# Two decode attentions on one core: the last sum in four strips with two stores, and the last rows of wo in three transfers

## The chip, the cores and the metric

The kernel runs on one core of a Trainium2 chip. Its time is the device time in microseconds of one launch. A run is also profiled; all durations below are of that one profiled execution, and they are compared with its own time.

## The reference

Two independent problems A and B of the same shape are computed and their results set side by side. Each is a decode step of attention with one query per batch entry: B = 2, D = 576, 32 query heads, 16 key/value heads of 128, a cache of 16384 positions of which the last W = 4096 are used.

```python
q = (x @ wq).reshape(B, 1, 32, 128).transpose(0, 2, 1, 3)
k = repeat(k_cache[:, :, Sk - W:, :], 2, axis=1)
v = repeat(v_cache[:, :, Sk - W:, :], 2, axis=1)
p = softmax(einsum("bhqd,bhkd->bhqk", q, k) * 128 ** -0.5)
o = einsum("bhqk,bhkd->bhqd", p, v)
return o.transpose(0, 2, 1, 3).reshape(B, 1, 4096) @ wo      # (2, 1, 576)
```

The output is `concatenate([a, b], axis=-1)`, bf16 of shape (2, 1, 1152). All inputs are bf16. The caches that are read, 4 times 33.5 MB, are nearly all of the 153 MB that the kernel moves.

## The kernel before

The kernel writes each engine's instruction order out by hand: `S.add(engine, fn, deps)` appends to that engine's list, and the dependencies become semaphore waits. All big transfers are issued by SyncE in one list, `stream`: wq of both problems, then per step one slab of K and one of V (4 MB each, for one group of heads of both batch entries), with the parts of wo set between them by `issue_wo`. A ring of four slabs, `ring`, takes them; a slab is issued when the slab four places earlier has been read.

A step `D_` (16 of them, `ND`, eight per problem) handles two key/value heads, one per batch entry: VectorE transposes the K slab into `xt` (L515), TensorE multiplies it with the masked queries `zq` into a score buffer `ST` (L540 and L188, which is the second matmul on weights that are already loaded), ScalarE takes the exponential (L585), VectorE transposes that into `pC` (L593), and TensorE multiplies `pC` with the V slab into `ACC` (L631, in four column strips of 32). Two steps make a group `G` (8 of them, `NG`), and a group's normalised output is multiplied with its rows of wo in `do_proj`. For all groups but the last (`by_group`), 512 of the 576 output columns are summed in PSUM tile `OT`, the other 64 in VectorE's `o_rest`.

The end of the kernel is the last group (`G` = 7, steps 14 and 15). `issue_slab` sends the last V slab in two pieces (L252), then `issue_wo(3)` the four head slices of step 14 (L291, 576 KB), and `issue_last` the rows of wo for the four heads of step 15: `HEADS = [(0, 1), (2,), (3,)]`, one transfer each of 288, 144 and 144 KB (L277), all into `wob`, each with its own semaphore `wl_sem`. All of these were issued by 332.3 us and wait in the transfer queues behind the slabs. Then SyncE issues the store of A's result `out_A` (L831), and last that of B's.

Before the last group, the sum so far is copied out of `OT` and `o_rest` into a part of a free score buffer, `fin(0)` (partitions 0 and 1, columns 0 to 287) and `fin(1)` (partitions 32 and 33, columns 512 to 799): `fin0` by ScalarE (L810), `fin1` and `fin2` by VectorE (L811, L813). The last group's matmuls add to it:

```python
for half in range(2):
    last = e.matmul(fin(half), l_, wob[:, w0 + s_, half * NH:(half + 1) * NH],
                    start=False, stop=end, skip_group_check=True)
```

Those of step 14 wait for `fin_ops`; those of step 15 are three parts (L778), each waiting for its own transfer of wo. In between stand three idle matmuls (`do_redist(3, 3)`), which compute nothing that is used. `do_E` then copies one half to bf16 by ScalarE (L822) and the other by VectorE (L823), both into `pR`, and `do_out` (L831) stores the two rows of 576 columns when both copies are done. SyncE waits for the stores (L985).

Of the kernel before, what the change touches and what calls it, by code (L numbers as in the profile page):

```python
# [7 lines left out]
ACTF = mybir.ActivationFunctionType  # L8
ALU = mybir.AluOpType
# [50 lines left out]
def build_kernel(nc, probs, out, cfg=None):  # L60
# [8 lines left out]
    NPROB = len(probs)  # L69
    Bb, _one, D = x0.shape  # L70
# [12 lines left out]
    ND = SPP * NPROB  # L83
# [5 lines left out]
    HH = HD // 2  # L89
    NXC = NFC + 2  # L90
    NOUT = wo0.shape[1]
    NH = NOUT // 2
    NB0 = 512
    NB1 = NOUT - NB0
    assert NOUT % 2 == 0 and 0 < NB1 <= NB0
    SCALE = float(Dh) ** -0.5
    ZW = 152
    BIG = -1.0e30
# [3 lines left out]
    NSW = 32  # L102
    unit_of = {G: u for u, (g0, n) in enumerate(UNITS) for G in range(g0, g0 + n)}
    HEADS = [(0, 1), (2,), (3,)]
    NPC = len(PIECES)

    def by_group(G):
        return G < NG - 1

    def wo_slot(G):  # L110
        return {0: 0, 1: 8, 2: 16, 3: 24, 4: 0, 5: 8, 6: 16, 7: 24}[G]

    es = ExitStack()
    with es:
# [3 lines left out]
        wob = sb("wob", [128, NSW, NOUT], BF16)  # L118
# [21 lines left out]
        pR = sb("pR", [128, 1024], BF16)  # L140
# [24 lines left out]
        o_rest = sb("o_rest", [Bb, NB1], FP32)  # L165
        ident_r = sb("ident_r", [128, 32], BF16)
        out_A = sb("out_A", [Bb, NOUT], BF16)
        out_sb = [out_A[:, :], pR[0:Bb, 0:NOUT]]
        ps = lambda name, shape: es.enter_context(nc.psum_tensor(name, shape, FP32))
        NTB = 2  # L170
        TB = [ps("tb%d" % i, [128, 512]) for i in range(NTB)]
        ST = [ps("st%d" % i, [128, 1024]) for i in range(2)]
        OT = ps("ot", [128, 512])
# [7 lines left out]
        x_sem = sem("xload")  # L181
        wl_sem = [sem("wl%d" % n_) for n_ in range(len(HEADS))]
        out_sem = sem("outdone")
        piece_sem = [sem("piece%d" % n_) for n_ in range(NPC)]

# [7 lines left out]
        S = _Sched()  # L193
        dma_count = {}

        def dma_op(eng, sem_h, n_dmas, fn, deps, tag):
            op = S.add(eng, fn, deps, tag)
            dma_count[sem_h] = dma_count.get(sem_h, 0) + 16 * n_dmas
            op.dma = (sem_h, dma_count[sem_h])
            return op  # L200
# [33 lines left out]
        wo_last = []  # L234
        qproj = {}
        proj = {}
# [34 lines left out]

        def issue_last(woP, lo, r0, deps):
            for n_, hs in enumerate(HEADS):
                def f(e, n_=n_, hs=hs):
                    t, r = divmod(hs[0], 2)
                    row = t * HH + r0 + 256 + 128 * r
                    return e.dma_start(wob[:, lo + 4 + hs[0]:lo + 4 + hs[0] + len(hs), :],  # L277
                                       woP[row:row + 128 * len(hs), :].rearrange("(h d) n -> d h n", d=128)).then_inc(wl_sem[n_], 16)
                wo_last.append(dma_op("sp", wl_sem[n_], 1, f, deps, "wl%d" % n_))

        def issue_wo(part):
            lo, n, r0, P, deps, Gs = (
# [42 lines left out]
        rest_add = {}  # L325
# [4 lines left out]
        e_ops = {}  # L330
# [429 lines left out]

        fin_ops = []

        def fin(half):
            return ST[(ND - 2) % 2][32 * half:32 * half + Bb, 512 * half:512 * half + NH]

        def do_proj(D_):
            G = D_ // 2
            P = G // GPP
            u = unit_of[G]
            s0 = 8 * (G - UNITS[u][0])  # L770
            w0 = wo_slot(G)
            new = G % GPP == 0
            if by_group(G):
                parts = [([(Rsb[u % 2][:, :, s0 + s_], s_) for s_ in range(8)], [r_ev[u], wo_dma[G]], new, True, True)]
            elif D_ < ND - 1:
                parts = [([(Rsb[u % 2][:, :, s_], s_) for s_ in range(4)], [r_ev[u], wo_dma[G]] + fin_ops, False, False, False)]
            else:
                parts = [([(oTn[:, h, :], 4 + h) for h in hs], [norm[D_], wo_last[n_]], False, False, n_ == len(HEADS) - 1)  # L778
                         for n_, hs in enumerate(HEADS)]
            for lhs, deps, start, rstart, rstop in parts:  # L780
                def f(e, rest, lhs=lhs, start=start, rstart=rstart, rstop=rstop):
                    last = None
                    for n_, (l_, s_) in enumerate(lhs):
                        begin, end = n_ == 0, n_ == len(lhs) - 1
                        if by_group(G):
                            first = e.matmul(OT[0:Bb, 0:NB0], l_, wob[:, w0 + s_, 0:NB0], start=start and begin, stop=end, skip_group_check=True)  # L786
                            last = matmul_again(e, first, rest[0:Bb, 0:NB1], wob[:, w0 + s_, NB0:NOUT], rstart and begin, rstop and end)
                        else:
                            for half in range(2):
                                last = e.matmul(fin(half), l_, wob[:, w0 + s_, half * NH:(half + 1) * NH],  # L790
                                                start=False, stop=end, skip_group_check=True)
                    return last
                deps = deps + [e_ops[(P - 1, 0)]]
                if by_group(G):
                    n, bank, proj[D_] = tb_job(f, "proj%d" % D_, deps)
                    rest_at[G] = bank
                    if G % GPP < GPP - 1 and G < NG - 2:
                        d = [proj[D_]]
                        if new:
                            if P:  # L800
                                d.append(e_ops[(P - 1, 1)])
                            rest_add[G] = S.add("dve", lambda e: e.tensor_copy(o_rest[:, :], bank[0:Bb, 0:NB1]), d, "rest%d" % G)
                        else:
                            d.append(rest_add[G - 1])
                            rest_add[G] = S.add("dve", lambda e: e.tensor_tensor(o_rest[:, :], o_rest[:, :], bank[0:Bb, 0:NB1], ALU.add),
                                                d, "rest%d" % G)
                        tb_consumer[n] = rest_add[G]
                    elif G == NG - 2:
                        d = [proj[D_], chain[(ND - 2, "exp")], chain[(ND - 2, "max")]]
                        a_ = S.add("act", lambda e: e.activation(fin(0), OT[0:Bb, 0:NH], ACTF.Copy), d, "fin0")  # L810
                        tb_consumer[n] = S.add("dve", lambda e: e.tensor_tensor(  # L811
                            fin(1)[:, NB0 - NH:NH], o_rest[:, :], bank[0:Bb, 0:NB1], ALU.add), d + [rest_add[G - 1]], "fin1")
                        fin_ops.append(S.add("dve", lambda e: e.tensor_copy(fin(1)[:, 0:NB0 - NH], OT[0:Bb, NH:NB0]), [a_], "fin2"))  # L813
                    else:
                        rest_at[G] = (n, bank)
                else:
                    proj[D_] = S.add("pe", lambda e, f=f: f(e, None), deps, "proj%d" % D_)

        def do_E(P):
            G = (P + 1) * GPP - 1  # L820
            if G == NG - 1:
                e_ops[(P, 0)] = S.add("act", lambda e: e.activation(out_sb[P][:, 0:NH], fin(0), ACTF.Copy), [proj[2 * G + 1]], "Elo%d" % P)  # L822
                e_ops[(P, 1)] = S.add("dve", lambda e: e.tensor_copy(out_sb[P][:, NH:NOUT], fin(1)), [proj[2 * G + 1]], "Ehi%d" % P)  # L823
                return
            n, bank = rest_at[G]
            e_ops[(P, 1)] = tb_consumer[n] = S.add("dve", lambda e: e.tensor_tensor(
                out_sb[P][:, NB0:NOUT], o_rest[:, :], bank[0:Bb, 0:NB1], ALU.add), [proj[2 * G + 1], rest_add[G - 1]], "Ehi%d" % P)
            e_ops[(P, 0)] = S.add("act", lambda e: e.activation(out_sb[P][:, 0:NB0], OT[0:Bb, 0:NB0], ACTF.Copy), [proj[2 * G + 1]], "Elo%d" % P)

        def do_out(P, c0, c1, eng, deps):  # L830
            dma_op(eng, out_sem, 1, lambda e: e.dma_start(  # L831
                out[:, 0, P * NOUT + c0:P * NOUT + c1], out_sb[P][:, c0:c1]).then_inc(out_sem, 16), deps, "out%d_%d" % (P, c0))

        init_mask()
        for i in range(NG // 2):
# [13 lines left out]
        for s in range(ND):  # L849
            D2 = s - 2  # L850
            c = s - 1
# [29 lines left out]
            if s in proj_at:  # L881
                do_proj(2 * proj_at[s] + 1)
                if proj_at[s] == GPP - 1:
                    do_E(0)
# [20 lines left out]
        do_comb(D_)  # L905
        do_norm(D_)
        do_proj(2 * 5 + 1)
        do_redist(2)
        do_comb(ND - 2)
# [9 lines left out]
        do_proj(ND - 2)  # L919
        do_proj(D_)  # L920
        do_E(NPROB - 1)
        for P in range(NPROB):
            do_out(P, 0, NOUT, "sp", [e_ops[(P, 1)], e_ops[(P, 0)]])

        S.check()

        for e in ENGS:
            n = 0
# [15 lines left out]
        while left:  # L944
            for e in ENGS:
                while idx[e] < len(S.ops[e]):
                    op = S.ops[e][idx[e]]
# [76 lines left out]
```

## Time and profile before

| | us |
|---|---|
| three runs | 362.78, 362.88, 363.33 (median 362.88) |
| the profiled execution | 363.02 |
| its span, first to last instruction | 361.8 |
| TensorE, VectorE, ScalarE, GpSimd busy | 218.6, 200.9, 68.2, 35.3 |
| transfers: 153.27 MB | 424 GB/s over the span |

How to read the views: in the slices of the page each digit is a share in tenths of one of 40 equal stretches of the span. In the chain of waits each line is a start, a duration, and the work (or the transfer) that the end of the kernel was waiting for at that time. In the timeline a line is start, duration, engine, source line, operation, destination and source with shape, number of instructions, and in brackets the idle time before and what ended it; `SPq` and `ACTq` are SyncE's and ScalarE's queues issuing transfers, `PEld` the weight loads of TensorE.

### The profile page before, as it was taken

To read this page: it belongs to the slowest core of one execution; us is meant where nothing else is said; L and a number is where in the kernel's file an instruction comes from. 1 tells how busy PE (TensorE), PEld (TensorE's weight loads), DVE (VectorE), ACT (ScalarE), POOL (GpSimd) and SP (SyncE) were. 2 spreads that over 40 slices of the span, in tenths; PEclk is the share of its full clock that TensorE was granted. 3 is DMA by queue.
4 is the path that set the end of the run, shared out by engine and by line. 5 is a ranking of instruction groups with operands and counts; after the bars stand their busy time and mean duration, and the time that the engine had idled before them with its cause. 6 is when DMAs were issued, how large, how long until landed. Compare 5 with 4: busy or idle time off the path is not lost.

```text
span 361.8 us, 2730 instructions
## 1 busy us (share of the span) xinstructions
PE 218.6 (60%) x1318; PEld 55.8 (15%) x945; DVE 200.9 (56%) x175; ACT 68.2 (19%) x149; POOL 35.3 (10%) x55
## 2 busy tenths in 40 slices
PE   0399195763747207466574737766867707657786
PEld 0010021120111101112120201212121201211132
DVE  4112599846647019283756658392919239079931
ACT  1036502130203002103020203020201203002131
POOL 1000000004000400001300040002100040200020
PEclk9999689997889857969698978899898978969999
DMA  8999999999999999999999999999999999999996
GB/s 348 421 449 406 464 406 437 431 408 453 415 442 438 428 424 438 429 428 438 417 446 422 435 428 442 426 435 428 424 424 440 431 424 433 431 438 428 438 409 248
DMA packets 6491, 153.27 MB, mean 424 GB/s; under 512 B 712, under 2 KB 1232, under 8 KB 1616
## 3 DMA queue, kind: packets, MB, share of 16 engines
q1 hardware_dynamic: 6476, 153.10, 98.8%
q8 instruction: 9, 0.15, 0.2%
q14 instruction: 2, 0.02, 0.0%
q10 hardware_dynamic: 4, 0.00, 0.0%
HBM read 153.10 MB, written 0.00 MB: 423 GB/s over the span
## 4 chain that ended last, share of the span: by engine, by line
DMA 72%; DVE 17%; PE 7%; ACT 3%; SPq 1%; issue 0%
DMA ring<-in_B_k_cache_dram 34%; DMA ring<-in_A_k_cache_dram 27%; DVE xt L515 14%; DMA wob<-in_B_wo_dram 8%; DMA wob<-in_B_x_dram 3%; PE st L188 3%; PE st L540 3%; ACT wob L465 1%; DVE wob L475 1%; ACT qk L483 1%; PE st L450 1%; DVE m L550 1%; ACT wob L470 1%; DVE nM L563 0%; SPq L252 0%
## 5 line engine op out<-in xcount | busy, mean ns | idle before, releaser
L515 DVE STREAM_TRANSPOSE xt<-ring 128x2048 f32<-128x2048 f32 x64 | 145.3, 2284 | 86.6 <-DMA ring<-in_A_k_cache_dram 49.8
L540 PE MATMUL st<-xt,zq 128*128 128x512 bf16 x256 | 111.6, 436 | 122.6 <-DVE xt L515 98.1
L188 PE MATMUL st<-xt,zq 128*128 128x512 bf16 x256 | 110.1, 430 | 0.0
L540 PEld LDWEIGHTS st<-xt,zq 128*128 128x128 bf16 x256 | 27.1, 106 | 216.3 <-DVE xt L515 113.5
L631 PE MATMUL acc<-ring,pC 128*32 128x512 bf16 x512 | 32.5, 381 | 1.2 <-DMA ring<-in_B_v_cache_dram 1.2
L568 ACT ACTIVATE nMrep<-nM 1x128 f32<-1x128 f32 x16 | 4.9, 308 | 146.9 <-DVE nM L563 146.9
L643 ACT ACTIVATE acc_sb<-acc 128x512 bf16<-128x512 f32 x16 | 9.5, 596 | 79.9 <-PE acc L631 79.9
L593 DVE STREAM_TRANSPOSE pC<-pR 128x1024 bf16<-128x1024 bf16 x16 | 19.6, 1223 | 3.7 <-ACT pR L585 2.1
L650 POOL TENSOR_TENSOR acc_sb<-acc_sb,masks 128x1024 bf16<-128x1024 bf16 (+1 forms) x8 | 13.4, 1679 | 66.6 <-ACT acc_sb L643 66.6
L550 DVE TENSOR_REDUCE m<-st 128x1 f32<-128x1024 f32 x16 | 19.0, 1190 | 1.4 <-PE st L188 1.4
L502 POOL TENSOR_TENSOR zq<-qk,masks 128x128 bf16<-128x128 bf16 x16 | 6.3, 398 | 136.2 <-PE st L188 114.4
L585 ACT ACTIVATE pR<-st,bias_sb 128x1024 bf16<-128x1024 f32 x16 | 17.8, 1114 | 0.5
L475 DVE STREAM_TRANSPOSE wob<-wob 128x512 f32<-128x512 f32 x8 | 5.7, 711 | 20.3 <-ACT wob L465 12.9
L415 ACT ACTIVATE st<-maskB 128x1024 f32<-128x1024 bf16 x16 | 16.5, 1032 | 1.6 <-POOL rsel L600 0.4
L786 PE MATMUL ot<-wob,Rsb 128*2 128x512 bf16 x56 | 15.2, 390 | 0.0
L631 PEld LDWEIGHTS acc<-ring,pC 128*32 128x32 bf16 x512 | 12.4, 96 | 15.9 <-issue 3.2
L600 POOL TENSOR_TENSOR rsel<-masks,rsum 128x16 f32<-128x16 bf16 x8 | 1.7, 216 | 108.0 <-ACT pR L585 108.0
L188 PE MATMUL tb<-wob,Rsb 128*2 128x64 bf16 x56 | 10.9, 195 | 0.0
L375 PE MATMUL tb<-wob 4*128 4x16 bf16 x5 | 0.3, 179 | 14.5 <-DVE wob L380 14.5
L653 POOL TENSOR_TENSOR acc_sb<-acc_sb 128x512 bf16<-128x512 bf16 (+1 forms) x8 | 8.2, 1029 | 0.6
L188 PE MATMUL st<-ring,wob 128*128 128x512 bf16 x24 | 7.9, 445 | 0.0
L579 ACT ACTIVATE bias_sb<-tb 128x1 f32<-128x1 f32 x16 | 2.7, 171 | 24.8 <-PE tb L573 24.8
(89 smaller groups left out, 99.5 us busy)
## 6 DMA issues: line engine op xcount, KB each, us to landing
ring<-in_A_k_cache_dram SPq DMA_DIRECT2D x8, 4096.0 KB, 30.4
ring<-in_A_v_cache_dram SPq DMA_DIRECT2D x8, 4096.0 KB, 32.5
ring<-in_B_k_cache_dram SPq DMA_DIRECT2D x8, 4096.0 KB, 28.4
ring<-in_B_v_cache_dram SPq DMA_DIRECT2D x7, 4096.0 KB, 32.8
wob<-in_A_wo_dram SPq DMA_DIRECT2D x1, 4608.0 KB, 43.3
ring<-in_A_wq_dram SPq DMA_DIRECT2D x1, 4096.0 KB, 12.7
ring<-in_B_wq_dram SPq DMA_DIRECT2D x1, 4096.0 KB, 22.6
ring<-in_B_v_cache_dram SPq DMA_DIRECT2D x1, 3072.0 KB, 25.5
```

The source lines that it names most:

```text
L188: return e.add_instruction(mybir.InstMatmult(name=nc.get_next_instruction_name(), engine=i.engine, ins=[e.lower_ap(rhs), i.ins[1]], outs=[ ...
L415: chain[(s, "fill")] = S.add("act", lambda e: e.activation(ST[s % 2][:, :].rearrange("k (h j) -> k h j", h=2), maskB[:].unsqueeze(1).broad ...
L475: chain[(G, "qtr")] = S.add("dve", lambda e: e.transpose(qtr[:].bitcast(FP32), qrow[:].bitcast(FP32)), evs, "qtr%d" % G)
L515: Xop[(s, u)] = S.add("dve", lambda e: e.transpose(xt[:, i % NKT, :].rearrange("k (j w) -> k j w", w=64), ring[:, n % NR, :].bitcast(FP32) ...
L540: first = last = e.matmul(bank, zq[:, p4, s % NZQ, w0:w0 + 128], mv, start=False, stop=stop, skip_group_check=True)
L550: chain[(s, "max")] = S.add("dve", lambda e: e.tensor_reduce(m1[:, 0:1], ST[s % 2][:, :], AX.X, ALU.max), d, "max%d" % s)
L585: chain[(s, "exp")] = S.add("act", lambda e: e.activation(pR[:, :], ST[s % 2][:, :], ACTF.Exp, bias=bias_sb[:, 0:1], scale=SCALE, accum_ou ...
L593: chain[(s, "pC")] = S.add("dve", lambda e: e.transpose(pC[:, s % NPT, :, :].rearrange("k j c -> k (j c)"), pR[:, :]), d, "pC%d" % s)
L631: last = e.matmul(ACC[32 * cb:32 * cb + 32, 0:512], pC[:, D_ % NPT, j0_:j0_ + 4, :].rearrange("k j c -> k (j c)"), ring[:, n % NR, j0_ * 1 ...
L643: acc_ev[D_] = S.add("act", lambda e: e.activation(acc_sb[:, D_ % 2, :], ACC[:, :], ACTF.Copy), d, "accev%d" % D_)
L650: t = S.add("pool", lambda e: e.tensor_tensor(v, v, maskJ[:].unsqueeze(1).unsqueeze(3).broadcast_to([128, l1 - l0, 4, 128]), ALU.mult), [a ...
L786: first = e.matmul(OT[0:Bb, 0:NB0], l_, wob[:, w0 + s_, 0:NB0], start=start and begin, stop=end, skip_group_check=True)
```

## The change

The last group's sum lies in four strips of 144 columns, at partitions 0, 32, 64 and 96 of the same score buffer (`fin(q)`, all in columns 0 to 143), instead of two halves of 288. Each head therefore takes four matmuls of 144 columns instead of two of 288. `fin0` becomes three copies by ScalarE; VectorE makes the fourth strip in two parts. `do_E` copies partitions 0 to 33 by ScalarE and 64 to 97 by VectorE, 144 columns each, and the result is stored by two transfers of four pieces of 288 B: row 0 by SyncE, row 1 by ScalarE. The last head's 128 rows of wo come by three transfers on one semaphore: rows 65 to 127, 14 to 64 and 0 to 13. A's store keeps its form.

```diff
-    NH = NOUT // 2
+    NQ = NOUT // 4
     HEADS = [(0, 1), (2,), (3,)]
+    SHARES = [[(0, 128)], [(0, 128)], [(65, 128), (14, 65), (0, 14)]]
-        out_sb = [out_A[:, :], pR[0:Bb, 0:NOUT]]
+        out_q = pR[:, 0:NQ]
         def issue_last(woP, lo, r0, deps):
             for n_, hs in enumerate(HEADS):
-                def f(e, n_=n_, hs=hs):
...
-                wo_last.append(dma_op("sp", wl_sem[n_], 1, f, deps, "wl%d" % n_))
+                for pa, pb in SHARES[n_]:
+                    def f(e, n_=n_, hs=hs, pa=pa, pb=pb):
+                        t, r = divmod(hs[0], 2)
+                        row = t * HH + r0 + 256 + 128 * r
+                        return e.dma_start(wob[pa:pb, lo + 4 + hs[0]:lo + 4 + hs[0] + len(hs), :], woP[row:row + 128 * len(hs), :].rearrange(
+                            "(h d) n -> d h n", d=128)[pa:pb]).then_inc(wl_sem[n_], 16)
+                    op = dma_op("sp", wl_sem[n_], 1, f, deps, "wl%d" % n_)
+                wo_last.append(op)
-        def fin(half):
-            return ST[(ND - 2) % 2][32 * half:32 * half + Bb, 512 * half:512 * half + NH]
+        fin_all = ST[(ND - 2) % 2]
+
+        def fin(q):
+            return fin_all[32 * q:32 * q + Bb, 0:NQ]
-                            for half in range(2):
-                                last = e.matmul(fin(half), l_, wob[:, w0 + s_, half * NH:(half + 1) * NH],
+                            for q in range(4):
+                                last = e.matmul(fin(q), l_, wob[:, w0 + s_, q * NQ:(q + 1) * NQ],
                                                 start=False, stop=end, skip_group_check=True)
-                        a_ = S.add("act", lambda e: e.activation(fin(0), OT[0:Bb, 0:NH], ACTF.Copy), d, "fin0")
+                        def f_fin(e):
+                            last = None
+                            for q in range(3):
+                                last = e.activation(fin(q), OT[0:Bb, q * NQ:(q + 1) * NQ], ACTF.Copy)
+                            return last
+                        a_ = S.add("act", f_fin, d, "fin0")
...
-                            fin(1)[:, NB0 - NH:NH], o_rest[:, :], bank[0:Bb, 0:NB1], ALU.add), d + [rest_add[G - 1]], "fin1")
-                        fin_ops.append(S.add("dve", lambda e: e.tensor_copy(fin(1)[:, 0:NB0 - NH], OT[0:Bb, NH:NB0]), [a_], "fin2"))
+                            fin(3)[:, NB0 - 3 * NQ:NQ], o_rest[:, :], bank[0:Bb, 0:NB1], ALU.add), d + [rest_add[G - 1]], "fin3")
+                        fin_ops.append(S.add("dve", lambda e: e.tensor_copy(fin(3)[:, 0:NB0 - 3 * NQ], OT[0:Bb, 3 * NQ:NB0]), [a_], "fin4"))
-                e_ops[(P, 0)] = S.add("act", lambda e: e.activation(out_sb[P][:, 0:NH], fin(0), ACTF.Copy), [proj[2 * G + 1]], "Elo%d" % P)
-                e_ops[(P, 1)] = S.add("dve", lambda e: e.tensor_copy(out_sb[P][:, NH:NOUT], fin(1)), [proj[2 * G + 1]], "Ehi%d" % P)
+                e_ops[(P, 0)] = S.add("act", lambda e: e.activation(out_q[0:32 + Bb, :], fin_all[0:32 + Bb, 0:NQ], ACTF.Copy), [proj[2 * G + 1]], "Elo%d" % P)
+                e_ops[(P, 1)] = S.add("dve", lambda e: e.tensor_copy(out_q[64:96 + Bb, :], fin_all[64:96 + Bb, 0:NQ]), [proj[2 * G + 1]], "Ehi%d" % P)
+        def do_out(P):
+            to = out[:, 0, P * NOUT:(P + 1) * NOUT]
+            if P < NPROB - 1:
+                parts = [("sp", to, out_A[:, :])]
+            else:
+                parts = [(eng, to[b, :].rearrange("(q c) -> q c", q=4), out_q[b:128:32, :]) for b, eng in enumerate(("sp", "act"))]
+            for n_, (eng, to_, src) in enumerate(parts):
+                dma_op(eng, out_sem, 1, lambda e, to_=to_, src=src: e.dma_start(to_, src).then_inc(out_sem, 16),
+                       [e_ops[(P, 1)], e_ops[(P, 0)]], "out%d_%d" % (P, n_))
```

More of the change, by code (lines that the diff above doesn't have):

```diff
@@ L91, in build_kernel @@
     NOUT = wo0.shape[1]
-    NH = NOUT // 2
+    NQ = NOUT // 4
     NB0 = 512
     NB1 = NOUT - NB0
-    assert NOUT % 2 == 0 and 0 < NB1 <= NB0
+    assert NOUT % 4 == 0 and 0 < NB1 <= NQ
     SCALE = float(Dh) ** -0.5
@@ L273, in issue_last @@
             for n_, hs in enumerate(HEADS):
-                def f(e, n_=n_, hs=hs):
[L275 to L278, printed above, removed]
-                wo_last.append(dma_op("sp", wl_sem[n_], 1, f, deps, "wl%d" % n_))
+                for pa, pb in SHARES[n_]:
[6 more added lines that the diff above has]
+                wo_last.append(op)
         def issue_wo(part):
@@ L826, in do_E @@
             e_ops[(P, 1)] = tb_consumer[n] = S.add("dve", lambda e: e.tensor_tensor(
[L827 to L832, printed above, removed]
+                out_A[:, NB0:NOUT], o_rest[:, :], bank[0:Bb, 0:NB1], ALU.add), [proj[2 * G + 1], rest_add[G - 1]], "Ehi%d" % P)
+            e_ops[(P, 0)] = S.add("act", lambda e: e.activation(out_A[:, 0:NB0], OT[0:Bb, 0:NB0], ACTF.Copy), [proj[2 * G + 1]], "Elo%d" % P)
+        def do_out(P):
[7 more added lines that the diff above has]
+                       [e_ops[(P, 1)], e_ops[(P, 0)]], "out%d_%d" % (P, n_))
         init_mask()
@@ L922, in build_kernel @@
         for P in range(NPROB):
-            do_out(P, 0, NOUT, "sp", [e_ops[(P, 1)], e_ops[(P, 0)]])
+            do_out(P)
         S.check()
```

## The prediction

> **What bounds the kernel now.** I read the page first, then its chain of waits, the DMA view cut to the last microseconds, and the timeline of the end. The page's slices:
>
> ```profile
> DMA  8999999999999999999999999999999999999996
> GB/s 348 421 449 406 464 406 437 431 408 453 415 442 438 428 424 438 429 428 438 417 446 422 435 428 442 426 435 428 424 424 440 431 424 433 431 438 428 438 409 248
> ```
>
> The 16 DMA engines are full in every slice but the first and the last: the transfers bound the kernel, and no engine's work before the last slice shortens it. The change touches only what follows the last transfers. The chain of waits, its end:
>
> ```profile
> 331.87 27.84 DMA wob<-in_B_wo_dram
> 359.71 0.04 issue
> 359.75 0.31 PE st L790 x2
> 360.06 0.02 issue
> 360.08 0.45 DVE pR L823
> ```
>
> The last transfer in the queue, 128 rows of wo for the last head (144 KB), lands at 359.71. Behind it stand, in series, two matmuls of 288 columns, VectorE's copy, and SyncE's store. The timeline of that stretch:
>
> ```profile
> 359.40 0.08 PEld L790 LDWEIGHTS st<-wob,oTn 128*2 128x2 bf16 x2 [0.22 <-DMA wob<-in_B_wo_dram]
> 359.75 0.08 PEld L790 LDWEIGHTS st<-wob,oTn 128*2 128x2 bf16 x2 [0.27 <-DMA wob<-in_B_wo_dram]
> 360.08 0.40 ACT L822 ACTIVATE pR<-st 2x288 bf16<-2x288 f32 x1 [1.88 <-PE st L790]
> 360.08 0.45 DVE L823 CAST pR<-st 2x288 bf16<-2x288 f32 x1 [1.37 <-PE st L790]
> 360.57 0.26 SPq L831 DMA_DIRECT2D out_dram<-pR  x1
> ```
>
> TensorE waits on each of the last two transfers of wo, and both copies start together. From the store's issue at 360.57 to the span's end at 361.8 is 1.2 us. The DMA view of 356 to 360, in slices of 0.1 us:
>
> ```profile
> DMA  9789999998989897667677656555933210000000
> ```
>
> The engines do not stop together: the share falls from about 357.4 to zero near 359.4 (the lone 9 is an instruction packet). The trace's semaphore arrivals give the steps. The next to last transfer of wo lands on five engines from 357.45 to 357.66, on three at 357.99, 358.41 and 358.47, and on eight from 358.84 to 359.36; the last transfer about 0.35 later on each. Every transfer of 128 rows is 8 rows on each of 16 engines; a row of 1152 B takes 0.047 us in the packet records, a transfer's closing 4 B packet 0.005.
>
> **The change part by part.** Profiled execution: 363.02 us, span 361.8 and 1.2 around it; the median is 362.88, 0.14 lower. I work out the difference on the profiled run and take it off the median.
>
> *The three transfers.* Bytes and their place behind the other heads stay; only which DMA engine carries which rows can change. Two more issues on SyncE cost 2 x 0.53 (1.58 for three in its row at 330.72), and out_A's store is moved past them. Nothing waits there: the rows start to flow some 25 us later, and out_A's store, landed at 359.01, is awaited only at the end.
>
> No row shows 63, 51 or 14 rows. What the trace shows are equal shares: 128 rows as 16 x 8, and out_A's two rows as one row on each of two engines (arrivals at 358.10 and 359.01). I take it that a transfer goes in equal shares to the most engines, up to 16, that divide its rows, always starting at the same engine: 63 is 9 x 7, 51 is 3 x 17, 14 is 14 x 1. The first three engines then carry 25 rows, the next six 8, the next five 1 and the last two none. The Trainium skill, "DMA: Bandwidth & Descriptors", section "Why a DMA increments its semaphore by 16 and not by 1", gives this rule and says that the lowest-numbered engines are used. The trace agrees for 2 and 128 rows.
>
> 25 rows in three transfers cost 25 x 0.047 + 3 x 0.005 = 1.19 after the landing of the head before. The two engines of out_A must be the first two; from out_A's arrivals one is among the five early ones, the other is the 358.47 one: 358.47 + 1.19 = 359.66. An engine with 8 rows ends as now, at most at 359.71; one with a single row at 359.36 + 0.05 = 359.41. So the last landing is 359.66 to 359.72 if the third engine is not late; I take 359.66, **-0.05**. Bounds: -0.30 (359.41) to +0.84 (359.36 + 1.19 = 360.55).
>
> *Matmuls.* Each head has four of 144 columns in four column strips in place of two of 288 in two. Now a pair of 288 starts every 0.12 and one takes 0.283, so 288 columns stream in 0.12 and 0.163 is latency. The PV matmuls in four strips ran 8 of 512 columns in 0.62, so four strips work side by side: the last head takes 0.163 + 0.06 + some 0.02 of issue, 0.24 against 0.31: **-0.06**. If the eight instructions of the last head (four loads, four matmuls) were paced one after the other it would be 0; bounds -0.07 to +0.05. The 16 for the head group before end near 358.9 and hide behind the landing at 358.97 of the last group's first wo transfer.
>
> *Early copies* (fin0 to fin4). ScalarE's 0.36 becomes three of 144 columns, 0.29 each by the slope below: +0.5. VectorE's 80 columns follow and end near 355.4 instead of 355.04. TensorE needs them at 357.48, after the last piece of V: 2 us of cover, cost nothing. Uncovered it would be 0.4.
>
> *Final copies.* VectorE: 0.449 for 288 columns and 0.222 for 64 give about 1.0 ns a column and 0.155 fixed; 144 columns: 0.30. ScalarE: 0.40 for 288 and 0.597 for 512, so about 0.28. 34 partitions instead of 2 cost nothing by the rows with 128. The later of the two falls from 0.45 to 0.30: **-0.15**.
>
> *Stores.* Each row of the output goes out as four pieces of 288 B, one row by SyncE, one by ScalarE. Both wait for both copies; ScalarE's new wait has nothing queued behind it. SyncE's issue takes 0.26 for two engines, 0.40 to 0.60 for 16, so about 0.30 for four. ScalarE issues once in the trace, the load of x:
>
> ```profile
> 0.79 0.53 ACTq L203 DMA_DIRECT2D wob<-in_A_x_dram  x1
> ```
>
> 0.53, and its first packet starts at 1.71, 0.92 behind the issue's start, where the store's first packet on SyncE (361.315) starts 0.75 behind. The later store sets the end: **+0.17** by that row; bounds -0.03 (shorter packets, same issue) and +0.27 (0.53 against 0.26). The same page of the Trainium skill, section "Specifications", says that a transfer under 512 B makes the engine read, modify and write, which speaks against pieces of 288 B. No row of before has such a store to HBM, and the page gives no price; the sum would be above mine by an unknown amount.
>
> Sum: -0.05 - 0.06 - 0.15 + 0.17 = **-0.09**: 362.93 for a profiled run, 362.8 for the median.
>
> **The rivals.** *Equalised end (faster side).* If the heavy shares fall only on engines that are done early, and the late ones get one row or none, the last landing is 359.41, and with stores at their better bound -0.30 - 0.06 - 0.15 - 0.03 = -0.54: 362.3. For it speaks the staircase, 1.9 us wide; against it out_A's arrival at 359.01, by which one of the first two engines is not early.
>
> *A late engine gets the 17 rows (slower).* If the third engine is one of the eight late ones, its landing is 358.84 to 359.36 plus 1.19, 360.03 to 360.55 in place of 359.71: +0.32 to +0.84, with the rest (-0.04) +0.28 to +0.80: 363.2 to 363.7. It decides as soon as that engine's landing of the head before is later than 359.71 + 0.04 - 1.19 = 358.56. For it: eight of the 14 engines outside out_A's two are. Against it: the late ones look like a block. The trace has nine 16 KB instruction packets (about 1.0 us each), eight of them before the end, each of which set one engine back for good; neither of out_A's two is in that group, so a block at the far end is as natural. The ninth packet, at 358.81, starts directly behind an engine's last row; between two shares of one engine it could add most of 1 us here.
>
> *The transfers spread evenly anyway.* 63, 51 and 14 rows over 16 engines are 6 to 9 rows each: last landing 359.66 to 359.80, -0.05 to +0.09. The shares then do nothing, and the copies and stores alone decide: -0.09 to +0.05, about 362.85.
>
> **How the numbers follow.** Chances: forecast 0.42, slower rival 0.30, equalised 0.15, even spread 0.13. About 0.2%, 0.73 us, is what a measurement of this kernel can tell from no change. The forecast and the even spread stay within it. The slower rival passes it where the third engine is one of the five latest (landing 359.15 to 359.36: +0.59 to +0.80) and the store or the instruction packet adds to it: 0.17, and 0.03 for a store much dearer than ScalarE's row: 0.20 slower. The equalised end reaches -0.54; beyond -0.73 something unlisted must help: 0.10 at most with the other cases. The rest, 0.70, is the same. The range goes from the equalised end, 362.3, to the slower rival's end, 363.7.
>
> **What would show it.** In the changed profile: the last landing of wo (359.66; 360.0 to 360.6 under the slower rival, 359.4 equalised), from it to the copies 0.26 to 0.30 instead of 0.37, copies of 0.30 and 0.28, and on the queues one store each by SyncE and ScalarE, the latter's issue at 0.3 to 0.5. The arrivals of the three transfers show the shares: 9, 3 and 14 engines, or 16 each. The forecast is wrong if the staircase of the engines ends elsewhere, or if from the stores' issue to the end takes over 1.5 us.

## The result: slower by about 0.3%, and the profile after

| | before | changed |
|---|---|---|
| median, 8 runs each | 362.78 | 364.11 |
| lowest to highest | 362.75 to 363.33 | 363.74 to 364.37 |
| profiled execution, its span | 363.02, 361.8 | 363.76, 362.5 |

The ratio is 1.0033, 95% interval 1.0024 to 1.0042: 0.9 to 1.5 us slower. The forecast was 362.8 in a range to 363.7.

The timeline of the end in the changed profile (columns as before):

```profile
359.85 0.09 PEld L795 LDWEIGHTS st<-wob,oTn 128*2 128x2 bf16 x4 [0.26 <-DMA wob<-in_B_wo_dram]
359.85 0.23 PE L795 MATMUL st<-wob,oTn 128*2 128x144 bf16 x4
360.13 0.28 ACT L832 ACTIVATE pR<-st 34x144 bf16<-34x144 f32 x1 [2.25 <-PE st L795]
360.14 0.31 DVE L833 CAST pR<-st 34x144 bf16<-34x144 f32 x1 [1.74 <-PE st L795]
360.50 0.61 ACTq L847 DMA_DIRECT2D out_dram<-pR  x1
360.51 0.64 SPq L847 DMA_DIRECT2D out_dram<-pR  x1
```

From TensorE's release to the copies it is 0.28 instead of 0.33, and the copies take 0.28 and 0.31 instead of 0.40 and 0.45. But each of the two stores takes 0.6 to issue where the one took 0.26, and from the issue to the span's end it is 1.97 us instead of 1.19. The strips gave 0.2, the stores took 0.8: that is the first loss.

The second loss lies ahead of these lines. The last piece of V is the last transfer that both kernels issue alike, so I count from there to each landing (the moment when the semaphore of a transfer has its last step). TensorE's weight loads of the kernel before, when the last piece of V and then the last rows of wo had landed:

```profile
356.87 0.12 PEld L631 LDWEIGHTS acc<-ring,pC 128*32 128x32 bf16 x8 [1.50 <-DMA ring<-in_B_v_cache_dram]
```

and the release at 359.75 that the prediction shows: 2.88 us. In the changed kernel:

```profile
356.55 0.12 PEld L634 LDWEIGHTS acc<-ring,pC 128*32 128x32 bf16 x8 [1.51 <-DMA ring<-in_B_v_cache_dram]
359.24 0.35 PEld L795 LDWEIGHTS st<-wob,oTn 128*2 128x2 bf16 x12 [0.75 <-issue]
```

and 359.85: 3.30 us, 0.42 more. V's own landing is 0.3 earlier in this profile. Over all profiles of this study it lies between 356.4 and 357.2, also among kernels that do not differ up to there, so that part is not the change's. Without it the two profiles differ by 0.42 up to the last rows of wo and, from their landing to the span's end, by 2.68 - 2.05 = 0.63: 1.04 together, in line with the ratio.

The DMA view of 356.5 to 360.5 in slices of 0.1 us, before and then changed:

```profile
DMA  9999898989766767765655593321000000000000
```
```profile
DMA  9899999785678797867565549100000000000000
```

In the packet records a row of wo takes 51 ns (at most 53) in the kernel before, but up to 142 in the changed one, and 80 in the mean between 0.75 and 1.0 us after V's landing. The heads *before* the divided one suffer too: the transfer of the head before lands 2.95 after V's instead of 2.53. The longer rows are only a part of the 0.42, though. The last packet ends 2.51 behind V's landing before and 2.66 in the changed kernel, 0.15 later; the other 0.27 lies between that end and the last landing, 0.37 before and 0.63 changed. In the kernels below this stretch is 0.37 to 0.40 wherever the last head comes as it did before, and 0.61 to 0.74 wherever its rows are divided.

### The profile page after: what moved, and what is told of

The parts are those of the page before. It is cut to its first block, busy times and chain, and to the rows that moved or that the text cites. A ratio compares the mean times of both kernels' runs of the same rounds, so it can differ in the third digit from the quotient of the medians.

```text
span 362.5 us, 2768 instructions
## 1 busy us (share of the span) xinstructions
PE 221.2 (61%) x1334; PEld 56.5 (16%) x961; DVE 200.7 (55%) x175; ACT 68.6 (19%) x151; POOL 35.3 (10%) x55
## 4 chain that ended last, share of the span: by engine, by line
DMA 71%; DVE 16%; PE 7%; ACT 3%; SPq 2%; issue 0%
DMA ring<-in_B_k_cache_dram 33%; DMA ring<-in_A_k_cache_dram 27%; DVE xt L518 14%; DMA wob<-in_B_wo_dram 7%; DMA wob<-in_B_wq_dram 4%; PE st L189 3%; PE st L543 3%; SPq L279 1%; ACT wob L468 1%; DVE wob L478 1%; ACT qk L486 1%; PE st L453 1%; DVE m L553 1%; ACT wob L473 1%; DVE nM L566 0%
## 5 line engine op out<-in xcount | busy, mean ns | idle before, releaser
L634 PE MATMUL acc<-ring,pC 128*32 128x512 bf16 x512 | 33.9, 394 | 1.8 <-DMA ring<-in_B_v_cache_dram 1.8
```

Source lines behind the costliest of these rows:

```text
L634: last = e.matmul(ACC[32 * cb:32 * cb + 32, 0:512], pC[:, D_ % NPT, j0_:j0_ + 4, :].rearrange("k j c -> k (j c)"), ring[:, n % NR, j0_ * 1 ...
```

## The experiments

Landings "behind V's" count from the last landing of the last piece of V, to about 0.01. In the eight profiles in which the last head comes in one transfer with its rows in order (the kernel before among them), the head before lands 2.47 to 2.54 behind V's and the last rows 2.83 to 2.91. Every timed kernel is given with its own comparison.

**1. The change in halves.** First, `SHARES[2]` back to one transfer, the strips and stores kept:

```diff
-    SHARES = [[(0, 128)], [(0, 128)], [(65, 128), (14, 65), (0, 14)]]
+    SHARES = [[(0, 128)], [(0, 128)], [(0, 128)]]
```

> The changed kernel with the last head's 128 rows of wo in one transfer again; strips, copies and the two stores stay. Theory S (most of the loss is the stores, 1.99 us from issue to end against 1.23; matmuls and copies give back 0.2): 362.8 + 0.76 - 0.22 = 363.3, store issues still 0.6 each. Rival T (the uneven transfers are the loss): 362.6, with the last landing of wo 0.35 after that of the head before, as in the kernel before.

Median 363.80 against 362.87, ratio 1.0023 (1.0014 to 1.0031), +0.8 us. Its timeline:

```profile
357.27 0.12 PEld L634 LDWEIGHTS acc<-ring,pC 128*32 128x32 bf16 x8 [1.51 <-DMA ring<-in_B_v_cache_dram]
360.16 0.09 PEld L795 LDWEIGHTS st<-wob,oTn 128*2 128x2 bf16 x4 [0.27 <-DMA wob<-in_B_wo_dram]
360.81 0.61 ACTq L847 DMA_DIRECT2D out_dram<-pR  x1
360.82 0.64 SPq L847 DMA_DIRECT2D out_dram<-pR  x1
```

From V to the last rows 2.89, as before the change; the long issues stay, and the end is at 362.87. Second, the kernel before with only the new `issue_last` and `SHARES`:

> The kernel before with only the last head's rows in three transfers of 63, 51 and 14 rows. Theory S: the transfers cost at most 0.4 (in the changed profile the last landing of wo is 3.31 behind that of the last piece of V, before 2.89): 362.8 to 363.2. Rival T: 363.6 to 364.1, nearly all of the loss. If the shares help as the change would have them, below 362.7.

Median 363.39 against 362.87, ratio 1.0011 (1.0002 to 1.0020), +0.4 us.

```profile
356.72 0.12 PEld L634 LDWEIGHTS acc<-ring,pC 128*32 128x32 bf16 x8 [0.52 <-DMA ring<-in_B_v_cache_dram]
360.16 0.08 PEld L793 LDWEIGHTS st<-wob,oTn 128*2 128x2 bf16 x2 [0.26 <-DMA wob<-in_B_wo_dram]
360.99 0.25 SPq L834 DMA_DIRECT2D out_dram<-pR  x1
```

3.44 from V to the last rows, a short issue. The two halves add up: 1.0023 and 1.0011 for the ratio 1.0033. That the stores are the larger part was expected, but each half costs more than it was given: the first came 0.5 above its 363.3, the second 0.2 above its 362.8 to 363.2.

**2. Why a store became long.** Three things changed at once: two queues at the same moment, four pieces instead of two, and partitions 32 apart. Both stores on SyncE (on the one-transfer kernel):

```diff
-... for b, eng in enumerate(("sp", "act"))]
+... for b, eng in enumerate(("sp", "sp"))]
```

> As the one-transfer kernel, but both stores of four pieces are issued by SyncE, one behind the other. If an issue is long (0.6 for 0.26) because two queues issue in the same moment, each takes 0.3 here and the end comes at the same time as or 0.1 to 0.3 before that of the two-queue kernel: 363.0 to 363.3. If a store of four pieces on four engines is dear by itself, the issues take 0.6 each in series and the end is 0.5 to 0.6 later: 363.8.

363.84 against 362.87, ratio 1.0026 (1.0016 to 1.0036). With no other queue issuing at that time, the two issues still take 0.64 and 0.55:

```profile
360.44 1.23 SPq L847 DMA_DIRECT2D out_dram<-pR  x2
```

Two queues with the old form of store (on the kernel before):

```diff
-            do_out(P, 0, NOUT, "sp", [e_ops[(P, 1)], e_ops[(P, 0)]])
+            if P < NPROB - 1:
+                do_out(P, 0, NOUT, "sp", [e_ops[(P, 1)], e_ops[(P, 0)]])
+            else:
+                do_out(P, 0, NH, "sp", [e_ops[(P, 1)], e_ops[(P, 0)]])
+                do_out(P, NH, NOUT, "act", [e_ops[(P, 1)], e_ops[(P, 0)]])
```

> The kernel before, but the result is stored as two halves of 288 columns (two pieces of 576 B on two engines each), one by SyncE and one by ScalarE, both waiting for both copies. If two queues that issue in the same moment hinder each other: issues of about 0.6, end 0.5 to 0.8 later, 363.3 to 363.6. If the four pieces are what is dear: issues of 0.26 to 0.3, 362.8; with ScalarE's own issue of 0.53 as in the load of x, 363.0.

363.15 against 362.87, ratio 1.0007 (0.9998 to 1.0017): not told from no change.

```profile
360.37 0.26 ACTq L831 DMA_DIRECT2D out_dram<-pR  x1
360.38 0.26 SPq L831 DMA_DIRECT2D out_dram<-pR  x1
```

Two issues at one moment take 0.26 each, ScalarE's no longer than SyncE's. From issue to end it is 1.33 against 1.19. So neither the two queues by themselves nor ScalarE made the stores dear; it is their form. The strips stored one by one, two pieces of 288 B from adjacent partitions each:

```diff
+                parts = [(("sp", "act")[q // 2], out[:, 0, P * NOUT + q * NQ:P * NOUT + (q + 1) * NQ], out_q[32 * q:32 * q + Bb, :],
+                          [e_ops[(P, q // 2)]]) for q in range(4)]
...
```

> As the one-transfer kernel, but the result is stored strip by strip: four stores of 2 pieces of 288 B on two engines, two by SyncE behind ScalarE's copy, two by ScalarE behind VectorE's. If small pieces are what is dear, issues stay near 0.6 each and the end is later than with one issue per queue: 364.2 or more. If it is the four engines, issues are 0.26: two in a row 0.55, the end 0.3 later than with one short issue, and the 0.22 from matmuls and copies is kept: 362.8 to 363.0, about as the kernel before.

363.13 against 362.84, ratio 1.0009 (1.0000 to 1.0017).

```profile
360.06 0.56 SPq L847 DMA_DIRECT2D out_dram<-pR  x2
360.10 0.63 ACTq L847 DMA_DIRECT2D out_dram<-pR  x2
```

About 0.3 an issue: pieces of 288 B are not what is dear. This expectation named the number of engines as the alternative; the next two show that it is the stride. The same four pieces per store, from four adjacent partitions, of which most do not hold the row that is stored, first one run and then ten:

```diff
-... out_q[b:128:32, :]) ...
+... out_q[64 * b:64 * b + 4, :]) ...
```

> As the one-transfer kernel, but each store takes its four pieces of 288 B from four adjacent partitions (0 to 3 and 64 to 67) instead of four that lie 32 apart; two of the three are not the output's, so the stored values are others. If the stride over partitions is what makes an issue 0.6, it falls to 0.26 to 0.35 and the end comes 0.4 to 0.7 earlier, 363.1 for a profiled run. If four pieces or four engines cost it, the issue stays 0.6 and the time at 363.4 to 364.2.

Issues of 0.279 each; 362.95 for the profiled run.

> The same kernel as the one with stores from adjacent partitions, now timed in rounds (two of the three further partitions are not the output's). If the stride is the whole of the store's excess, it stands where the strips' gain of 0.2 and a second store's 0.13 leave it: 362.8 to 362.9, and 0.9 below the kernel with one transfer and strided stores. If the second store costs as much as in the two half stores (+0.28), 363.0.

362.93 against 362.83, ratio 1.0006 (0.9997 to 1.0016).

```profile
360.25 0.28 ACTq L847 DMA_DIRECT2D out_dram<-pR  x1
360.25 0.28 SPq L847 DMA_DIRECT2D out_dram<-pR  x1
```

And the stride alone, with two pieces of 1152 B, one store and none of the other edits (the second piece is not the result's row):

```diff
+            src = out_sb[P][:, c0:c1] if P == 0 else pR[0:64:32, c0:c1]
...
```

> The kernel before, but the last store takes its two pieces of 1152 B from partitions 0 and 32 instead of 0 and 1; row 1 of the stored result is not the output's. If a stride over partitions makes an issue long by itself, the issue is 0.4 to 0.6 instead of 0.26 and the end 0.3 to 0.6 later, 363.2 to 363.4. If it takes four pieces or small ones as well, no difference: 362.85.

363.34 against 362.83, ratio 1.0015 (1.0006 to 1.0024).

```profile
360.37 0.62 SPq L832 DMA_DIRECT2D out_dram<-pR  x1
```

The same two pieces on two engines take 0.62 instead of 0.26 to issue, and 1.69 instead of 1.19 to the end. Source partitions 32 apart instead of adjacent are the cause; that is shown with two pieces and with four. Other steps were not run, and what in the issue the stride lengthens, no run shows.

The packet records split the 0.8 of the changed kernel. Before, the store's first piece starts 0.74 behind the start of the issue; from partitions 0 and 32 it is 1.26. In the changed kernel ScalarE's pieces start 1.26 behind their issue too, but SyncE's, issued at the same moment, 1.52 (1.61 in the one-transfer kernel). From adjacent partitions both stores start 0.76 to 0.78 behind. So about 0.5 is the stride of one store, and about 0.26 comes from a second strided store beside it: with this form the two queues do matter. Why the second one waits, no run shows.

**3. Why dividing the rows of wo hurts.** On the kernel before, two even transfers, `[(64, 128), (0, 64)]`, 8 rows per engine as always:

> The kernel before with the last head's rows in two transfers, 64 to 127 and 0 to 63, so 4 rows of each on every DMA engine: 8 rows per engine as with one transfer. Theory P (rows that arrive at other partitions than an engine's usual ones, while slower engines still write, hold those up): the rows of the heads before are stretched again and the last landing is over 2.9 behind that of V, up to 3.4; 363.0 to 363.4. Rival H (the 25 rows on three engines are the loss): 2.88 + 0.01, 362.87.

363.40 against 362.84, ratio 1.0012 (1.0002 to 1.0021).

```profile
356.50 0.12 PEld L634 LDWEIGHTS acc<-ring,pC 128*32 128x32 bf16 x8 [1.21 <-DMA ring<-in_B_v_cache_dram]
359.29 0.08 PEld L793 LDWEIGHTS st<-wob,oTn 128*2 128x2 bf16 x2 [0.17 <-DMA wob<-in_B_wo_dram]
359.88 0.08 PEld L793 LDWEIGHTS st<-wob,oTn 128*2 128x2 bf16 x2 [0.51 <-DMA wob<-in_B_wo_dram]
```

3.38 with an even load: the 25 rows on three engines are not needed for the loss. The head before lands 2.80 behind V's. The three sizes at other places, `[(0, 63), (63, 114), (114, 128)]`:

> The kernel before with three transfers of the same sizes, 63, 51 and 14 rows, but for other partitions: 0 to 62, 63 to 113, 114 to 127. The load of each DMA engine is the same as in the change. Rival H (load): the last landing stays 3.3 to 3.45 behind V's, 363.4. Theory P (which partitions are written early): the 63 rows no longer go where the late engines write, the 51 on three engines do; the stretch is smaller, 2.9 to 3.2 behind V's, 362.9 to 363.2.

363.44 against 362.84, ratio 1.0016 (1.0007 to 1.0025), 3.28 behind V's: hardly better. Going by which partitions are written early, I had expected 2.9 to 3.2 and at most 363.2; with the load as the cause, 363.4, which is where it came. The even load of the run before speaks against the load as the whole of it, so this miss stays unexplained. The division by columns, where every engine keeps its rows:

```diff
+                for ca, cb in ([(0, NOUT)] if n_ < len(HEADS) - 1 else [(0, NH), (NH, NOUT)]):
...
```

> The kernel before with the last head's rows in two transfers by columns: all 128 rows of columns 0 to 287, then of 288 to 575. Every engine keeps its own rows and partitions and has 8 pieces of each transfer. Theory P (rows at other partitions than an engine's usual ones hold others up): no stretch, landing 2.88 to 2.95 behind V's, 362.9. Rival N (a further transfer on the queue is dear by itself, whatever its rows): 3.3 or more behind V's, 363.3.

362.92 against 362.83, ratio 1.0002 (0.9993 to 1.0012).

```profile
356.48 0.12 PEld L633 LDWEIGHTS acc<-ring,pC 128*32 128x32 bf16 x8 [1.50 <-DMA ring<-in_B_v_cache_dram]
359.53 0.08 PEld L792 LDWEIGHTS st<-wob,oTn 128*2 128x2 bf16 x2 [0.38 <-DMA wob<-in_B_wo_dram]
```

3.04 behind V's, a little over the 2.88 to 2.95 that I expected, for twice the pieces; no row of the heads before takes over 53 ns and each half row of the last head takes 29. The head before lands at 2.58. A further transfer is not what stretches the rows. One transfer of 128 rows with its source rows taken in another order:

```diff
+                        src = woP[row:row + 128, :].rearrange("(j i) n -> i j n", i=16)
...
```

> The kernel before with the last head's 128 rows in one transfer whose source rows are taken 8 apart (row 16 j + i of wo to partition 8 i + j), so that the rows of wo stand in another order and the result is another one. Theory R (the stretch comes from which rows of HBM an engine reads, or from which partitions it writes once the rows are shared out otherwise): rows over 51 ns and a landing 3.1 to 3.4 behind V's with a single transfer. If only the further transfers matter, 2.88 behind V's and rows of 51 ns.

One run, 363.25: 3.04 behind V's, less than the 3.1 to 3.4 that I expected, the head before at 2.79 instead of 2.53, rows up to 128 ns. A single transfer of the same load stretches as soon as its rows are dealt out otherwise. The last pair tells reading from writing: the same rows read by the same engines, both halves written to partitions 0 to 63, or both to 64 to 127 (so that half of the last head's sum is of stale rows).

```diff
+                        slot = lo + 4 + hs[0] if half else 0
+                        return e.dma_start(wob[0:64, slot, :], woP[row + 64 * half:row + 64 * half + 64, :]).then_inc(wl_sem[n_], 16)
...
```

> The kernel before with the last head's rows in two transfers of 64 rows, first rows 64 to 127 of wo and then 0 to 63, both written to partitions 0 to 63 (the second into a slot that is free by then), so that the last head's product uses stale rows for half of its sum. Every engine reads the same rows as in the kernel that writes both to the high half. Theory W (the stretch is on the writing side, at the partitions where the late engines write): one of the two kernels, low or high, is free of it (2.53 from V's last landing to that of the head before) and the other has more of it than the 2.80 of the 64 and 64 rows. By which engines write where in a full transfer I cannot tell which; the changed kernel, whose 63 early rows went to partitions 65 to 127, points to the high half as the bad one. Theory R (which rows of HBM an engine reads): both kernels the same, 2.8.

```profile
356.72 0.12 PEld L636 LDWEIGHTS acc<-ring,pC 128*32 128x32 bf16 x8 [0.57 <-DMA ring<-in_B_v_cache_dram]
359.37 0.08 PEld L795 LDWEIGHTS st<-wob,oTn 128*2 128x2 bf16 x2 [0.21 <-DMA wob<-in_B_wo_dram]
360.03 0.08 PEld L795 LDWEIGHTS st<-wob,oTn 128*2 128x2 bf16 x2 [0.57 <-DMA wob<-in_B_wo_dram]
```

> As the low one, but both transfers are written to partitions 64 to 127. Theory W: 2.8 to 3.2 from V's last landing to that of the head before, rows of over 70 ns, 363.4 to 363.8, while the low one stays at 2.53 to 2.6 and 362.9 to 363.1. Theory R: the same as the low one, 2.8.

```profile
356.56 0.12 PEld L636 LDWEIGHTS acc<-ring,pC 128*32 128x32 bf16 x8 [1.27 <-DMA ring<-in_B_v_cache_dram]
359.75 0.08 PEld L795 LDWEIGHTS st<-wob,oTn 128*2 128x2 bf16 x2 [0.39 <-DMA wob<-in_B_wo_dram]
360.16 0.08 PEld L795 LDWEIGHTS st<-wob,oTn 128*2 128x2 bf16 x2 [0.33 <-DMA wob<-in_B_wo_dram]
```

To the head before: 2.65 (low) against 3.19 (high), and in the packet records a mean row of 71 against 92 ns between 0.75 and 1.0 us after V. The times: 363.18 against 362.82, ratio 1.0009 (1.0000 to 1.0019), and 363.56 against 362.82, ratio 1.0020 (1.0011 to 1.0030). With the same reads the place of writing makes the difference: 0.54 at the head before, of the high kernel's 0.66, is on the writing side. The low one is not free of it, as I had expected of one of the two (2.53 to 2.6, and at most 363.1). At the last rows the difference is smaller: 3.31 (low) and 3.60 (high) behind V's, so that the low kernel keeps 0.42 of delay. Most of that comes behind the head before: 0.66 from there to the last rows, where it was 0.35. What this part is stays open. The times go the same way, but their two intervals overlap.

No version beat the kernel before. The adjacent stores, which do not store the result, and the division by columns come nearest and are not told from it.

## Why the prediction was wrong

**Stores: the step that failed most.** I bounded them by ScalarE's load of x (0.53 to issue) and took +0.17, at most +0.27; they cost +0.8, about 0.5 for the stride of one store and the rest for two such stores at once. ScalarE's row was the wrong neighbour: its issues at the end take 0.26 to 0.28. What counted was in the edit and in no row: a source of partitions 32 apart. I noted the four pieces and engines and passed over the stride. The prediction gave a store much dearer than ScalarE's row a chance of 0.03, and its sign of being wrong, over 1.5 us from the issue to the end, came with 1.97. A second store of the old form costs about 0.14 by the view and at most 0.6 by the interval.

The Trainium skill's read-modify-write under 512 B ("DMA: Bandwidth & Descriptors", section "Specifications") is not what made the stores dear. From issue to end the two stores of 288 B pieces from adjacent partitions take 1.38, the two of 576 B pieces 1.33: by the trace, the price of small pieces is at most about 0.05 here.

**Transfers: right shares, wrong cost.** The equal shares were right: the semaphore of the changed kernel is stepped by 9 + 3 + 14 = 26 landings, and once at each issue. But I let every engine run at its old 47 ns a row and counted loads alone: -0.05, with +0.84 only if a late engine got the 17 rows. (The 47 is what eight rows and a closing packet leave between the landings of two transfers, 0.38; the packet records themselves show 51.) The loss of 0.42 (0.56 in the transfers alone) comes with even loads too (0.50). The step that failed is the assumption that a division of rows costs nothing as long as no engine gets more than its load: rows and landings stretch, also those of the heads before, and by the last pair of runs the place of writing has a large part in it. The reading that fits is that early engines, sent to other partitions than their usual ones, hold up those that are still writing there, and that the staircase (the uneven finish of the engines, 1.9 us wide) makes this possible. That is argued, not shown: no record here says which engine writes where, no run has the division without the staircase, and the three sizes at other places and the rest of the low kernel's delay do not follow from it. The Trainium skill has a piece that would fit this reading: "SBUF — State Buffer", section "SBUF: two separate sides", names the DMA ports of SBUF as a place where several DMA engines contend, and "DMA: Bandwidth & Descriptors", section "The descriptor swizzle", gives each engine of a full transfer one port of its own, the upper half of the engines on partitions 64 to 127. The trace has the high half as the worse one, 3.19 against 2.65 at the head before; it does not number the engines or the ports, so whether the ports are what they contend for, no run here shows.

**Matmuls and copies: right.** -0.05 for the forecast -0.06, -0.14 for -0.15. The early copies end at 354.62, not near 355.4, since this profile starts them 0.66 earlier and three take 0.75 rather than 0.86; their cover of 2 us was there.

**The rivals.** The slower end came, by another way: the late engine with 17 rows is refuted as the needed cause, and so is the instruction packet: it runs from 358.95 to 360.04, when the last rows had landed at 359.81, so none of them stood behind it. The equalised end did not come: the landings of the head before, which no share touches, already came 0.42 later. The range ended at 363.7 because it held an unseen form of store to the issue of a seen one, and because it let a division of rows cost nothing as long as no engine had more than its load.

## What to carry to other kernels

A store whose source steps over partitions is a form of its own (here steps of 32; loads and other steps were not run): measure it before a layout makes it necessary, for the 0.2 us that four strips give back is less than the 0.5 by which one such store ends later. When the end of a kernel waits for the DMA engines, as here, keep the division of rows over them that a full 128-partition transfer has; if one must be divided, divide its columns. An uneven finish of the DMA engines is not free room by itself: every division of rows that was tried to use it or beside it landed later.

## What the runs showed of the hardware that was not expected

- A store of two pieces takes 0.26 us to issue from adjacent partitions and 0.62 from partitions 0 and 32; with four pieces 0.28 and 0.55 to 0.64. Two such strided stores issued at once do not start together: the second one's pieces come 0.26 to 0.35 later still.
- When the 128 rows are divided over transfers, a row can take up to 142 ns instead of 51 in the changed kernel (153 with the three sizes at other places), and the last landing comes 0.61 to 0.74 behind the last packet instead of 0.37 to 0.40.
- An issue can take very long while transfers are queued ahead of it. In the changed kernel:

```profile
330.31 18.90 SPq L279 DMA_DIRECT2D wob<-in_B_wo_dram  x5
349.26 2.47 SPq L847 DMA_DIRECT2D out_dram<-out_A  x1
```

Of these 18.9 us the transfer of 51 rows on three engines took 2.76 and the 14 rows after it 14.56. The kernel before, with no transfer of so few engines, has no issue over 1.1 us in that stretch; what the two wait for, no run shows. I had costed them at 0.53 each and called them hidden. They were: the 14 rows were issued some 8 us before they could flow, and A's store landed at 359.87, over 2 us before the end. Here the cover is what made a mistake of 16 us cost nothing.
